# A sliding-window attention branch rewritten with transposed probabilities, 64-row score tiles, list scheduling and early weights on the SyncE queue

## The chip, the cores and the metric

One core of a Trainium2 chip. The metric is the device time of one execution in microseconds (us); executions of one kernel agree within about 1% here. Engine names: PE is TensorE (PEld the loading of its weights), DVE VectorE, ACT ScalarE, POOL GpSimd, SP SyncE.

## The reference, cut to what matters

Two branches read the same input and are mixed by a gate.

```python
g = sigmoid((x * gate_w).sum(-1, keepdims=True))          # x: 1 x 2048 x 640
a = A_ref(x, wqkv, wo)      # 32 heads of 20, each query sees itself and 255 keys before it
b = B_ref(x, mem0, Wq, Wk, Wv, Wo, seg_len=32)   # 64 segments in sequence, 32 heads of 192, 8 memory rows
return g * a + (1 - g) * b
```

The change touches branch A alone, and how branch B's weights get into the chip while A runs.

## The kernel before

It has four stages: branch A over 16 query blocks of 128 rows; projections of the tails for branch B; the recurrence of branch B; the mix. Branch A walks the heads in a fixed order. Scores stand with queries on the partitions, so the probabilities must be transposed on PE and evacuated before they meet V:

```python
def st_scores(h):
    for ci, c in enumerate(kbs):                       # up to 3 key blocks
        nc.tensor.matmul(sp[...], lhsT=qm[r][:, g, :], rhs=kring[c][:, g, :], start=True, stop=not need_mask)
        if need_mask:                                  # 2 of the 3
            nc.tensor.matmul(sp[...], lhsT=ident[:], rhs=(m_last if c == qb else m_first)[:], start=False, stop=True)
    nc.vector.tensor_reduce(out=nmx[:], in_=sp[:, 0:nk * P], axis=AX.X, op=ALU.max, negate=True)
    nc.scalar.activation(out=ex[:, 0:nk * P], in_=sp[:, 0:nk * P], func=ACT.Exp, bias=nmx[:], scale=1.0)

def st_transpose(h):                                   # two heads at a time
    nc.tensor.transpose(pt_ps[:, a, ci, :], ex[:, ci * P:(ci + 1) * P], ident[:])
    ...                                                # copied out by ACT or DVE in turn
# ... values, output projection ...
early, late, last = weights.resident[:34], weights.resident[34:-3], weights.resident[-3:]
units = [lambda u=u: weights.load_resident(pre, u, nc.gpsimd) for u in early]
units += [lambda u=u: weights.pack(u, nc.gpsimd) for u in streamed]
```

`qm` are copies of Q in which all but one of four heads are zero. A "unit" loads one 384 KB weight tile of branch B, or packs one from DRAM to DRAM for later streaming; those of Wo are packed by four DMAs of 80 KB.

## Time and profile before

| stage | from, us | to, us | what limits it |
|---|---|---|---|
| branch A | 0 | 526 | order of coupled engines, PE most loaded |
| tail projections | 526 | 706 | PE, with one long store |
| recurrence | 706 | 2541 | PE and streamed weights |
| mix | 2541 | 2571 | small |

The median was 2569.75 us of 3 runs. The stage bounds are starts of the first instruction of a stage in the trace. The lines that carry the reading are in the prediction below.

### The profile page before, as it was taken

The page shows a single profiled execution, that of the slowest core. Times are in us where ns is not written, and L with a number is a line of the kernel's source. Part 1 is how long each engine was busy: PE and PEld are TensorE (multiplying, and loading weights), DVE is VectorE, ACT ScalarE, POOL GpSimd, SP SyncE. Part 2 cuts the span into 40 slices and gives each one's busy share as a digit, 9 for nine tenths or more (in the row PEclk, how much of TensorE's full clock was granted, in tenths as well). Part 3 has the DMA queues.
Part 4 walks back from the last instruction along what each step waited for, and adds up shares of the span by engine and source line. Part 5 has one row for each costly group of instructions (what it writes and reads, how often), then busy time and mean ns, then how long its engine had stood idle before and what let it go on. Part 6 is the DMA issues. An engine that isn't in the chain of part 4 may idle for free.

```text
span 2571.1 us, 114087 instructions
## 1 busy us (share of the span) xinstructions
PE 2226.3 (87%) x49877; PEld 1645.7 (64%) x49893; DVE 1198.7 (47%) x3578; ACT 1124.3 (44%) x2433; POOL 702.2 (27%) x1973
## 2 busy tenths in 40 slices
PE   7889888889889888888888888888888888889885
PEld 5777777679456665666656666656666566566663
DVE  5777777623234443444444344434443344344434
ACT  4777777622234333433333343333333343333333
POOL 7622222040122222222222222222222222222220
PEclk9999999899999999999999999999999999999996
DMA  6600000075578888888888888888888888888887
GB/s 210 202 17 18 17 17 15 9 252 148 144 242 277 265 263 263 276 266 278 269 259 269 271 275 266 264 256 270 265 266 270 255 268 273 268 266 270 268 258 228
DMA packets 293747, 561.63 MB, mean 218 GB/s; under 512 B 104568, under 2 KB 114048, under 8 KB 293248
## 3 DMA queue, kind: packets, MB, share of 16 engines
q1 hardware_dynamic: 266032, 495.28, 60.5%
q0 software_dynamic: 24256, 55.62, 7.3%
q8 instruction: 391, 6.41, 1.0%
q10 hardware_dynamic: 2960, 3.44, 0.4%
q14 instruction: 108, 0.88, 0.1%
HBM read 524.83 MB, written 36.51 MB: 218 GB/s over the span
## 4 chain that ended last, share of the span: by engine, by line
PE 53%; DMA 33%; ACT 9%; DVE 2%; issue 2%; SPq 0%; ACTq 0%; POOL 0%; DVEq 0%
DMA t_w<-w_packed 30%; PE ps_o L771 8%; PE ps_k L601 7%; PE ps_q L601 7%; PE ps_v L601 6%; ACT a_ex L195 4%; PE t_psum L440 4%; ACT a_pt L208 3%; PE qk_ps L124 3%; PE ps_pv L747 3%; PE tr_k L616 2%; PE t_psv L457 2%; PE S_ps L673 1%; PE pt_ps L205 1%; PE s_ps L187 1%
## 5 line engine op out<-in xcount | busy, mean ns | idle before, releaser
L601 PEld LDWEIGHTS <-t_hT 128*32 128x32 bf16 x15360 | 381.5, 98 | 292.3 <-issue 70.3
L771 PE MATMUL ps_o<-t_OT,t_w 128*128 128x40 bf16 x7040 | 290.5, 180 | 116.0 <-DMA t_w<-w_packed 108.7
L771 PE MATMUL ps_o<-t_OT,w_o 128*128 128x40 bf16 x8320 | 320.8, 180 | 48.0 <-ACT t_OT L752 45.2
L771 PEld LDWEIGHTS <-t_w 128*128 128x128 bf16 x7040 | 226.3, 96 | 136.9 <-DMA t_w<-w_packed 133.5
L771 PEld LDWEIGHTS <-w_o 128*128 128x128 bf16 x8320 | 267.0, 96 | 58.0 <-issue 48.4
L195 ACT ACTIVATE a_ex<-s_ps,a_nmx 128x384 bf16<-128x384 f32 (+2 forms) x512 | 252.8, 576 | 64.4 <-DVE a_nmx L193 64.2
L648 POOL COPY t_K<-t_xqk 128x64 bf16<-128x64 bf16 x256 | 60.9, 238 | 779.6 <-PE S_ps L673 779.6
L193 DVE TENSOR_REDUCE a_nmx<-s_ps 128x1 f32<-128x384 f32 (+2 forms) x512 | 247.0, 523 | 34.7 <-PE s_ps L190 25.4
L601 PE MATMUL ps_v<-w_v,t_hT 128*32 128x384 bf16 x4864 | 254.6, 337 | 0.1
L752 ACT CAST t_OT<-ps_pv 128x480 bf16<-128x480 f32 x256 | 143.2, 559 | 251.6 <-PE ps_pv L747 247.9
L601 PE MATMUL ps_q<-w_q,t_hT 128*32 128x384 bf16 x4096 | 223.0, 340 | 18.7 <-DVE t_hT L782 18.4
L639 DVE COPY t_K<-tr_k 128x256 bf16<-128x256 bf16 x256 | 74.6, 291 | 344.7 <-PE tr_k L616 344.4
L601 PE MATMUL ps_k<-w_k,t_hT 128*32 128x384 bf16 x4096 | 221.8, 339 | 0.0
L606 ACT CAST t_tok<-ps_k 128x384 bf16<-128x384 f32 x256 | 122.7, 479 | 206.3 <-PE ps_k L601 206.3
L625 ACT COPY b_QT<-tr_q 128x384 bf16<-128x384 bf16 x256 | 123.3, 482 | 180.1 <-PE tr_q L616 180.1
L730 DVE TENSOR_TENSOR t_PTx<-PT_ps,mk_x 128x320 bf16<-128x320 f32 x256 | 125.9, 492 | 153.2 <-PE PT_ps L723 153.1
L606 ACT CAST t_tok<-ps_q 128x384 bf16<-128x384 f32 x256 | 122.6, 479 | 145.8 <-PE ps_q L601 145.8
L683 DVE TENSOR_REDUCE sm_mx<-S_ps 128x4 f32<-128x160 f32 x256 | 82.2, 321 | 209.6 <-PE S_ps L673 209.0
L187 PE MATMUL s_ps<-KT_blk,QTm 128*128 128x128 bf16 x1440 | 172.0, 224 | 5.8 <-ACT a_ex L195 5.4
L606 ACT CAST t_vtok<-ps_v 128x384 bf16<-128x384 f32 x256 | 122.7, 479 | 103.7 <-PE ps_v L601 103.7
L561 POOL DMA_DIRECT2D t_xqk<-xbqk x256 | 137.4, 537 | 84.0 <-POOL b_QT L629 39.1
L205 PE MATMUL pt_ps<-a_ident,a_ex 128*128 128x128 bf16 x1440 | 146.4, 221 | 8.3 <-ACT a_ex L195 1.0
(138 smaller groups left out, 4469.2 us busy)
## 6 DMA issues: line engine op xcount, KB each, us to landing
t_w<-w_packed SPq DMA_DIRECT2D x704, 320.0 KB, 4.2
t_w<-w_packed SPq DMA_DIRECT2D x576, 384.0 KB, 4.4
xbqk<-t_qk SPq DMA_DIRECT2D x16, 768.0 KB, 4.3
t_xqk<-xbqk POOLq DMA_DIRECT2D x256, 48.0 KB, 3.7
w_v<-in_B_Wv_dram POOLq DMA_DIRECT2D x19, 384.0 KB, 8.2
w_q<-in_B_Wq_dram POOLq DMA_DIRECT2D x16, 384.0 KB, 5.2
w_k<-in_B_Wk_dram POOLq DMA_DIRECT2D x16, 384.0 KB, 6.9
xbv<-t_vt SPq DMA_DIRECT2D x64, 96.0 KB, 1.8
```

The source lines that it names most:

```text
L187: nc.tensor.matmul(sp[:, ci * P:(ci + 1) * P], lhsT=qm[r][:, g, :], rhs=kring[c][:, g, :], start=True, stop=not need_mask)
L193: nc.vector.tensor_reduce(out=nmx[:], in_=sp[:, 0:nk * P], axis=AX.X, op=ALU.max, negate=True)
L195: nc.scalar.activation(out=ex[:, 0:nk * P], in_=sp[:, 0:nk * P], func=ACT.Exp, bias=nmx[:], scale=1.0)
L205: nc.tensor.transpose(pt_ps[:, a, ci, :], ex[:, ci * P:(ci + 1) * P], ident[:])
L440: nc.tensor.matmul(pt[:, bb, :], lhsT=ws[ki][kt][:, c:c + P], rhs=xTb[:, kt, t * P:(t + 1) * P], start=(kt == 0), stop=(kt == KT - 1))
L561: sc.op("DMA", 500, lambda: nc.gpsimd.dma_start(tile_of(qk)[:].rearrange("p i b t -> p (i b t)"), xbqk[s, :, g].rearrange("p i c -> p (i c ...
L601: nc.tensor.matmul(t[32 * j:32 * j + 32, 0:384], lhsT=tile_of(hT)[:, kt, :], rhs=w[:, j * 384:(j + 1) * 384], start=(kt == kts[0]), stop=( ...
L606: sc.op("ACT", act(384), lambda: nc.scalar.copy(tile_of(tok)[:], b["tile"][:, 0:384]), reads=[b], writes=[tok])
L625: nc.scalar.copy(dst, tq["tile"][:].rearrange("p b (j t) -> p b j t", t=SEG))
L730: nc.vector.tensor_tensor(out=tile_of(dst)[:], in0=PT["tile"][:, i, :, :].unsqueeze(2).to_broadcast([P, 2, 4, L]), in1=mk.unsqueeze(1).uns ...
L752: sc.op("ACT", act(480), lambda: nc.scalar.copy(tile_of(OT)[:].rearrange("p b j l -> p (b j l)"), o["tile"][:, 0:480]), reads=[o], writes= ...
L771: nc.tensor.matmul(t[:, dt * L:(dt + 1) * L], lhsT=w[:, r * D + dt * P:r * D + (dt + 1) * P], rhs=OT["tile"][:, b, i, :], start=(g == 0 an ...
```

## The change

Its intent: compute the scores twice. The first pass has queries on the partitions and gives only the maximum of each row; the second has keys on the partitions, so that its exponentials are already the transposed probabilities that the value matmul wants as weights. The maximum is put into Q as two additional rows through an augmentation matmul. Heads lie in pairs within 64 rows, so that a score matmul uses half of PE's rows; each matmul of the first pass is issued next to one of the second, 22 heads behind, in the other half. All of branch A goes through the list scheduler that branch B had: a part of the program that takes the operations with their estimated lengths and, of those that are ready, emits the one of highest rank next.

```diff
-    nc.tensor.matmul(sp[...], lhsT=qm[r][:, g, :], rhs=kring[c][:, g, :], ...)
-    nc.tensor.matmul(sp[...], lhsT=ident[:], rhs=(m_last ...)[:], start=False, stop=True)
-    nc.vector.tensor_reduce(out=nmx[:], in_=sp[...], axis=AX.X, op=ALU.max, negate=True)
-    nc.tensor.transpose(pt_ps[:, a, ci, :], ex[...], ident[:])
+    nc.tensor.matmul(T(out)[:, i * P:(i + 1) * P], lhsT=b if keys_first else a, rhs=a if keys_first else b,
+                     start=True, stop=True, tile_position=(r, 0))          # r = 64 * (h % 4 // 2)
+    nc.vector.tensor_tensor_reduce(out=T(junk)[:, 0:n], in0=T(s)[:, 0:n], in1=mask[...], op0=ALU.add, op1=ALU.max, ...)
+    nc.scalar.activation(out=T(pt)[:, h % 4, 0:n], in_=T(s)[:, 0:n], func=ACT.Exp)
+    nc.gpsimd.affine_select(out=v, in_=v, compare_op=op, fill=0.0, ...)    # the mask, 2 for 4 heads
 ...
+    sc = Sched(..., make, stay=300)
+    LAG1, LAG2, BURST, AUG = 22, 30, 2, 2
 ...
-    early, late, last = weights.resident[:34], weights.resident[34:-3], weights.resident[-3:]
-    units = [lambda u=u: weights.load_resident(pre, u, nc.gpsimd) for u in early]
+    early, late, last = weights.resident[:29], weights.resident[29:-3], weights.resident[-3:]
+    units = [lambda sc, u=u: sc.op("DMA", 500, lambda: weights.load_resident(pre, u, nc.sync)) for u in early]
+    units += [lambda sc, u=u: sc.op("DMA", 500, lambda: weights.pack(u, nc.sync)) for u in streamed]
```

## The prediction

> **What bounds the kernel now.** I first split the span into stages by busy time per stretch; each engine name is followed by its busy microseconds and its instruction count.
>
> ```profile
> 0.00:60.00 60.00, 41.95 (x556) 33.54 (x558) 32.09 (x100) 27.86 (x78) 46.27 (x90) 0.94 0.63 201
> 60.00:100.00 40.00, 35.36 (x556) 28.88 (x554) 30.39 (x72) 30.49 (x64) 23.60 (x48) 0.96 0.80 276
> 100.00:500.00 400.00, 350.82 (x5687) 298.53 (x5698) 295.44 (x650) 293.96 (x562) 97.90 (x211) 0.94 0.09 24
> 526.00:706.00 180.00, 162.31 (x2240) 140.32 (x2239) 50.78 (x81) 43.20 (x80) 39.50 (x89) 0.97 0.65 187
> 706.00:2550.00 1844.00, 1608.40 (x40483) 1124.04 (x40483) 762.90 (x2630) 702.08 (x1607) 494.98 (x1537) 0.97 0.84 265
> ```
>
> The columns are PE, PEld, DVE, ACT, POOL, granted clock, DMA share and GB/s. The sliding branch takes the first 526 us, the projections of the tails the next 180, the memory recurrence 1844, the final mix about 20. The change rewrites only the first stage and its hand-off to the second. The page's chain is dominated by work of the recurrence, so it says nothing about this change; 526 us is all that can shrink.
>
> Inside the first stage I read the groups of instructions, shapes kept apart, between 100 and 500 us (some 12.5 query blocks):
>
> ```profile
> L195 ACT ACTIVATE a_ex<-s_ps,a_nmx 128x384 bf16<-128x384 f32 x391 | 201.3, 596 | 53.7 <-DVE a_nmx L193 53.5
> L193 DVE TENSOR_REDUCE a_nmx<-s_ps 128x1 f32<-128x384 f32 x392 | 199.5, 548 | 29.9 <-PE s_ps L190 21.4 <-remote 5.1 <-issue 0.2
> L187 PE MATMUL s_ps<-KT_blk,QTm 128*128 128x128 bf16 x1176 | 138.0, 225 | 4.2 <-ACT a_ex L195 4.2
> L205 PE MATMUL pt_ps<-a_ident,a_ex 128*128 128x128 bf16 x1169 | 114.0, 221 | 5.9
> L190 PE MATMUL s_ps<-m_first,a_ident 128*128 128x128 bf16 x392 | 88.4, 226 | 0.0
> L190 PE MATMUL s_ps<-m_last,a_ident 128*128 128x128 bf16 x392 | 88.1, 225 | 0.0
> L208 ACT COPY a_pt<-pt_ps 128x768 bf16<-128x768 bf16 x98 | 79.6, 812 | 25.4 <-PE pt_ps L205 25.0
> ```
>
> Per head there are 3 score, 2 mask and 3 transpose matmuls, one maximum, one exponential and half an evacuation of transposes. The durations overlap, so cost is better taken from start-to-start spacing in the trace: 56 ns for a 128-column matmul, 25 ns for the 21-column value matmuls. A block then needs on PE (96 + 64 + 96 + 80 + 10) x 56 = 19.4, values 96 x 25 = 2.4, V and output projections 2.7, together 24.6 us. The chain of waits shows what a block really takes:
>
> ```profile
> 262.94 2.44 PE out_ps L255 x9
> ...
> 278.63 0.81 ACT a_pt L208
> 279.49 0.31 PE o_ps L221 x6
> ...
> 286.44 1.91 ACT a_ex L195 x4
> ...
> 295.50 0.63 PE out_ps L255
> ```
>
> The same output projection returns after 32.6 us, and in between the chain hops PE, ACT, DVE. DVE and ACT are each busy about 74%. So no engine is full: the stage is bound by a fixed order of coupled engines with PE the most loaded (24.6 of 31 to 33 us).
>
> **What the Trainium skill says.** "TensorEngine Tiling (Array Packing)", Key Properties: a change of tiling mode drains TensorE, and tiles run in parallel. The trace agrees: a 128-row transpose followed by a column-tiled matmul starts 149 ns later instead of 56, and column-tiled score matmuls of the recurrence start 3 ns apart. Row tiles, which the change uses, do not occur before; "TensorE: Matmul & The Clock Gate", Measured speedup vs the span model, gives 3.07x for four. "VectorE: DVE Perf Modes", the perf-mode tier table, gives tensor_tensor no speed-up with a PSUM operand; the recurrence's 320-element one is spaced 407 ns, which agrees (333 at one element a cycle plus 74). "DMA: Bandwidth & Descriptors", HWDGE ordering: descriptors of one queue are consumed in ring order on each DMA engine. No row of the kernel before tests this, and my largest correction rests on it.
>
> **The change part by part.** Scores are computed twice, by query for the maximum and by key for the probabilities. This removes mask matmuls, probability transposes, their evacuations and the eight zero-padded Q tiles. The maximum goes back into Q through an augmentation matmul; masking goes into the DVE reduction and into POOL selects.
>
> PE per full block: 96 pairs of 64-row matmuls, the partners in opposite row halves, at 56 + 3 = 59 ns: 5.7; values 2.4; Q and K projections 80 x 56 = 4.5; V and output 2.7; transposes 0.6; augmentation 2 x (216 + 4 x 56) = 0.9; gate 0.1. That is 16.9. The order of instructions of the new kernel has 32 to 48 mode changes in a full block (counted from its PE list); 40 at about 95 ns (149 - 56, rounded up) are 3.8. PE: 20.7 us.
>
> DVE: the maximum is now an operation on two tensors, written as two instructions: 407 + 64/0.96 = 474, plus about 66 for the small second one (the spacing of one-column operations before): 540. Times 32: 17.3. K copies 0.9, normalisation 1.2, the rest 0.8: 20.2 us.
>
> ACT: an exponential without a bias tile is spaced 221 ns at 160 elements in the recurrence, so 221 + 224/1.2 = 408 at 384 (463 to 475 before). Times 32: 13.1. Evacuations of Q, K, V, augmented Q and outputs: 5.1. Together 18.2 us, from about 23.
>
> POOL: 16 selects of 512 elements at about 0.6 us (its 512-element copy took 0.61) plus 2.7: 12.3 us, not critical.
>
> Three engines sit between 18 and 21 us. A list-scheduled order with deeper buffers will not fill one wholly; the recurrence, ordered this way, keeps PE about 87% busy (1608 of 1844). I choose 23.5 us per full block, 88% of the PE sum.
>
> **The opening** matters as much. In the new SyncE order, input blocks 0 and 1 are followed by 29 weight loads of 384 KB, 9 packings of 384 KB and 44 of 80 KB, and only then by input block 2. That is 11.4 + 3.5 + 3.6 = 18.5 MB. The new PE order transposes input block 2 after only some 24 heads of block 0, and PE is in order, so everything stops there. About 3.6 MB of inputs go first, by 12 us (the first 10 us before moved 255 GB/s). Weight loads then at some 320 GB/s (268 at a DMA share of 0.84, scaled to a full share): 36 us; packings between DRAM places at an estimated 250 to 280: 27 us. Input block 2 lands near 75 us, while PE reaches it near 30. In the kernel before these weights went through POOL's queue and the input did not wait behind them.
>
> **Sum of the stage:** 75, plus 20 for the rest of blocks 0 and 1, plus 14 x 23.5 = 329, plus 14 for the drain (exponentials lag the maxima by 22 heads, 9 us, then values and output) = 438 us, against 526: minus 88.
>
> **Hand-off.** Five fewer resident weights are early (29, not 34), so 5 x 384 KB = 2 MB more load after the stage. The chain there shows
>
> ```profile
> 526.09 6.87 PE t_psum L440 x120
> 532.96 0.02 issue
> 532.99 0.59 ACT t_qk L445
> 533.58 0.02 issue
> 533.60 21.03 DMA xbqk<-t_qk
> ```
>
> a small-packet store that takes 21 us while the late weights load, against 4.3 us in the median. At 380 GB/s (the busiest late-load stretch) 2 MB are 5 us more of that crowd; I count 4. The new order of resident weights puts all Q and K but three early, as before, so no other wait appears. The recurrence and the mix keep their instructions.
>
> Total: 2570 - 88 + 4 = 2486 us.
>
> **Rivals.**
> 1. Row halves do not overlap. Then scores cost 192 x 56 = 10.8 instead of 5.7 and PE needs 26 us per block, some 28.5 in practice: plus 14 x 5 = 70, so 2556, within 2%. For it: no row tile in this trace. Against: column tiles overlap here, and partners use different PSUM banks.
> 2. The wait for input block 2 is short or hidden. PE reaches it at 30, so 45 us of wait are at stake; blocks 0 and 1 then run at once and the stage ends near 400: 2448. Against: the SyncE order is explicit.
> 3. The two-instruction maximum is dearer, say 650 ns: DVE becomes the bound at 23.7 and the block 26: plus 35, so 2521.
> 4. The schedule fits so well that PE's 20.7 becomes 21.5: minus 28, so 2458.
> 5. The gain is lost at the hand-off because the late loads crowd more stores: at most one further 21 us store, 2507.
>
> **Range and chances.** Rivals 2 and 4 set the low end, 2445; rival 3 with some of 5 sets the high end, 2535. Faster by over 2% means below 2518, which needs 52 us of the 84 to survive. Rivals 1 and 3 break it: 0.82 faster, 0.16 within 2%, 0.02 slower.
>
> **What would show it.** In the changed kernel: the stage ends near 440 and a full block recurs after 23 to 24 us; PE idles from about 30 to 75 us on the input's DMA; two score matmuls of a pair start a few ns apart; the maximum is spaced about 540 ns on DVE, the exponential about 410 on ACT; the first store of the tail projections still takes about 20 us. The prediction is wrong if pairs are spaced 56 ns each, if DVE is over 95% busy in steady blocks, or if input block 2 lands before 50 or after 100 us.

## The result

The changed kernel took 2500.43 us in the median of 4 runs (2485.29 to 2505.54), the kernel before 2573.47 in the median of 4. The ratio is 0.971, with an interval of 0.966 to 0.976. A ratio here is the mean time of one kernel's fast runs over that of the other's of the same rounds, so not quite the ratio of the medians. In a second set of rounds the unchanged file gave 2495.12 us and 0.969.

Busy time by stretch of the changed kernel (columns as in the prediction):

```profile
0.00:60.00 60.00, 18.08 (x225) 14.26 (x225) 18.45 (x70) 9.08 (x18) 17.78 (x54) 0.79 0.92 334
100.00:400.00 300.00, 286.97 (x5437) 208.90 (x5464) 262.88 (x1020) 249.51 (x577) 168.51 (x367) 0.99 0.09 24
640.00:2460.00 1820.00, 1587.62 (x40135) 1111.12 (x40135) 754.14 (x2599) 694.99 (x1589) 487.36 (x1513) 0.97 0.84 266
```

Branch A ends at 435.8 us instead of 526.1. In its middle PE is now busy 96%, DVE 88% and ACT 83%. The first 60 us are the opposite: PE is busy 18 us of 60, while the DMA engines are full. The recurrence is as it was.

The groups of instructions in the middle, 100 to 400 us, shapes kept apart:

```profile
L356 DVE CUSTOM_DVE_ANT_0 a_junk<-p_s,a_mask 128x384 bf16<-128x384 f32 x431 | 224.5, 553 | 33.9 <-PE p_st L326 26.0 <-PE p_s L326 0.9
L386 ACT ACTIVATE a_pt<-p_st 128x384 bf16<-128x384 f32 x408 | 184.1, 495 | 30.2 <-PE p_st L326 26.7 <-PE p_s L326 0.5
L326 PE MATMUL p_s<-a_k,a_q 64*128 64x128 bf16 x1299 | 130.5, 220 | 0.0
L394 POOL TENSOR_SCALAR_AFFINE_SELECT a_pt<-a_pt 128x512 bf16<-128x512 bf16 x211 | 130.0, 640 | 96.3 <-ACT a_pt L386 95.4
L326 PE MATMUL p_st<-a_qa,a_k 64*128 64x128 bf16 x1276 | 127.1, 218 | 5.8 <-ACT a_pt L386 4.5
L356 DVE DVE_READ_ACCUMULATOR2_ANT a_mx<- 128x1 f32 x431 | 35.4, 82 | 0.0
```

What idles DVE and ACT most is now PE's scores (26.0 of 33.9 and 26.7 of 30.2 us); before, ACT waited for DVE and DVE for PE's scores. The maximum is indeed two instructions.

The opening on the chain of waits, in order of time (start, length, what):

```profile
36.02 8.23 DMA w_packed<-in_B_Wq_dram
44.26 7.74 DMA w_packed<-in_B_Wv_dram
52.55 0.59 SPq L530
...
75.09 0.59 SPq L530
75.80 2.48 DMA a_xt<-in_A_x_dram
78.32 0.71 PE p_m L247 x5
```

The 0.59 us pieces are SyncE issuing one packing DMA of Wo after the other. Only then does it issue the load of input block 2, which lands in 2.48 us and lets PE go on. PE had come to a stop at about 32 us. The hand-off at the end of the stage:

```profile
435.77 7.51 PE t_psum L576 x120
443.28 0.02 issue
443.30 0.60 ACT t_qk L581
443.89 0.02 issue
443.91 26.66 DMA xbqk<-t_qk
```

The same store as before, now 26.66 us instead of 21.03.

The last stretch of the stage, in which only the drain is left, ran at a low granted clock (the third figure from the end):

```profile
400.00:435.00 35.00, 27.62 (x342) 18.08 (x344) 12.01 (x44) 21.16 (x46) 13.32 (x24) 0.55 0.02 6
```

### The profile page after: what moved, and what is told of

The parts are those of the page before. It is cut to its first block, busy times and chain, and to the rows that moved or that the text cites. A ratio compares the mean times of both kernels' runs of the same rounds, so it can differ in the third digit from the quotient of the medians.

```text
span 2483.5 us, 112898 instructions
## 1 busy us (share of the span) xinstructions
PE 2129.7 (86%) x49059; PEld 1521.8 (61%) x49093; DVE 1133.4 (46%) x3942; ACT 1047.4 (42%) x2385; POOL 745.7 (30%) x2097
## 4 chain that ended last, share of the span: by engine, by line
PE 56%; DMA 36%; ACT 3%; issue 2%; SPq 1%; DVE 1%; POOL 0%; ACTq 0%; DVEq 0%; POOLq 0%
DMA t_w<-w_packed 31%; PE ps_k L737 8%; PE ps_q L737 8%; PE ps_o L907 7%; PE ps_v L737 6%; PE t_psum L576 4%; PE p_s L326 3%; PE p_m L281 3%; PE ps_pv L883 2%; PE tr_k L752 2%; PE p_o L410 2%; PE S_ps L809 1%; PE t_psv L593 1%; PE p_st L326 1%; PE tr_q L752 1%
## 5 line engine op out<-in xcount | busy, mean ns | idle before, releaser
L356 DVE CUSTOM_DVE_ANT_0 a_junk<-p_s,a_mask 128x384 bf16<-128x384 f32 (+2 forms) x512 | 253.5, 528 | 45.0 <-PE p_st L326 32.9
L386 ACT ACTIVATE a_pt<-p_st 128x384 bf16<-128x384 f32 (+2 forms) x512 | 220.4, 474 | 89.9 <-PE p_st L326 81.1
L394 POOL TENSOR_SCALAR_AFFINE_SELECT a_pt<-a_pt 128x512 bf16<-128x512 bf16 x240 | 148.0, 639 | 124.5 <-ACT a_pt L386 123.5
L326 PE MATMUL p_st<-a_qa,a_k 64*128 64x128 bf16 x1440 | 150.7, 224 | 10.6 <-ACT a_pt L386 7.3
```

The source lines that it names most:

```text
L326: nc.tensor.matmul(T(out)[:, i * P:(i + 1) * P], lhsT=b if keys_first else a, rhs=a if keys_first else b, start=True, stop=True, tile_posi ...
L356: sc.op("DVE", 135 + n / 0.96, lambda: nc.vector.tensor_tensor_reduce(out=T(junk)[:, 0:n], in0=T(s)[:, 0:n], in1=mask[:, NKB * P - n:], op ...
L386: sc.op("ACT", act_ns(n), lambda: nc.scalar.activation(out=T(pt)[:, h % 4, 0:n], in_=T(s)[:, 0:n], func=ACT.Exp), reads=[s], writes=[pt])
L394: nc.gpsimd.affine_select(out=v, in_=v, compare_op=op, fill=0.0, base=0, pattern=[[0, 4], [sign, P]], channel_multiplier=-sign)
```

## The experiments

Runs e0_after to e4_early24 (none is called e3) were on one chip and e5_spread7 to e8_poolq on another, each set with the kernel before in its own rounds, so totals across the two sets are compared by their ratios.

A rival of the whole gain is the granted clock, which the views above give as 0.94 in the middle of branch A before and 0.99 after. The clock records of the traces settle it: TensorE was granted half its clock in stretches of 3.4 to 6.8 us, 44 of the 400 us before, and in none between 103 and 396 us after. Where no such stretch fell (102 to 195 us), a block before took 31.1 us, so only some 0.7 us of its mean of 31.8 is clock, against a gain of 9.6.

The theory: the gain is the shorter block, which PE bounds and which rests on row halves running side by side; the opening gives some 46 us away to the order on SyncE; the hand-off gives away 5. Rivals: DVE or ACT bound the block; the opening is not exposed, or it is the choice of queue and not of place; the store's time has nothing to do with late weights. The bounds of stages below are read from the traces, and the block's length is that between the transposes of input blocks 4 and 14, over 10.

**Control, e0_after.** No edit.

> Control: the changed kernel as it is. About 2500 us, ratio to before 0.971. In its profile input block 2 is transposed at about 78 us, the stage ends at about 436 us, a full block recurs every 22.4 us. If its clock is lower than in the first profile, the difference of 15 us between its own runs should lie in the stages with dense matmuls and not in the opening.

Measured: 2495.12 us, ratio 0.969. Input block 2 was transposed at 78.4 us, the stage ended at 435.8, a block took 22.19 us: to 0.1 us what the first profile had. The recurrence took 1838.5 us here and 1831.7 there. The tail projections took 188.4 us and 186.2. So the scatter of one kernel lies behind branch A, mostly in the recurrence, and the bounds within branch A can be compared to a fraction of a us as long as no stretch of half clock falls between them. I had expected the opening to be the same, but had tied the scatter to all dense matmuls; those of branch A had no part in it.

**The order of the early weights, e1_spread.** Each load is ordered behind the operation in front of it in the program. This changes only the emitted order; no wait is added.

```diff
-    units = [lambda sc, u=u: sc.op("DMA", 500, lambda: weights.load_resident(pre, u, nc.sync)) for u in early]
+    units = [lambda sc, u=u: sc.op("DMA", 500, lambda: weights.load_resident(pre, u, nc.sync), after=sc.ops[-1:]) for u in early]
```

and the same for `pack`.

> Only the place of the early weight loads in the SyncE order is changed: each is ordered behind the operation in front of it, so they spread over the stage and input block 2 no longer queues behind 18.5 MB. Theory (the opening wait is exposed time): PE does not stop at input block 2, the stage ends near 390 us, total 44 to 48 us less than the unchanged one, about 2454. Rival (the wait is only where the first blocks' latency shows; without it DMA traffic beside the blocks or POOL's tiles take the time back): less than 20 us gained.

Measured: 2444.26 us, ratio 0.948 (0.943 to 0.953), 51 us less than the control in the same rounds. Input block 2 was transposed at 31.7 us instead of 78.4, and the stage ended at 386.6 instead of 435.8. The first 50 us of it, by stretch:

```profile
0.00:50.00 50.00, 35.37 (x484) 25.89 (x484) 32.74 (x147) 21.45 (x63) 25.50 (x73) 1.00 0.39 125
```

PE is busy 35 of 50 us. A block took 22.19 us as before, with loads beside it. The opening was fully exposed time, and traffic beside the blocks cost them nothing that shows. The rival falls. The program tells why the weights had been bunched: it adds a unit every few heads, but a DMA operation without inputs is ready at time 0 for the scheduler, which then emits all of them at the start.

**Row halves, e2_samerows.**

```diff
-        LAG1, LAG2, BURST, AUG = 22, 30, 2, 2
+        LAG1, LAG2, BURST, AUG = 24, 30, 2, 2
```

> The lag between the two score passes is 24 heads instead of 22, so that both partners of a pair use the same half of the rows and cannot run side by side. Theory (overlap of row halves carries the gain on PE, and PE is the bound of a block): partners start 53 to 56 ns apart instead of 3 to 4, PE's sum per block rises by 96 x 52 ns = 5.0 us, a full block takes 26 to 28 us, total +50 to +75, about 2560, so nearly all of the gain over before is gone. Rival (blocks are bound by DVE and ACT, PE has slack): a block below 24 us, total below +25.

Measured: 2550.66 us, ratio 0.991 (0.985 to 0.996). Partners start 56 ns apart in the median (middle half 55 to 66) instead of 4 (3 to 38). A block took 26.73 us, 4.5 more; the stage ended at 494.8, 59 later, of which under 1 us is the drain of two more heads. The middle of the stage, and the same up to and from the block at which the granted clock falls:

```profile
100.00:400.00 300.00, 297.70 (x4671) 227.13 (x4671) 231.34 (x870) 218.31 (x494) 139.65 (x317) 0.94 0.08 21
126.00:277.00 151.00, 149.79 (x2462) 115.13 (x2459) 120.72 (x453) 114.34 (x256) 74.42 (x168) 1.00 0.08 22
277.00:392.00 115.00, 114.19 (x1652) 86.07 (x1652) 81.11 (x304) 78.09 (x173) 49.97 (x112) 0.85 0.07 19
```

PE is full and DVE's and ACT's shares fall. Not all of the 4.5 us is the lost overlap. At full clock, between input blocks 4 and 10, a block took 25.3 us, 3.1 more than the control's 22.3 there; from block 10 to 14 it took 28.8, with two stretches of half clock, 34 us together, of which the control had none. Whether the fuller PE brings them is not shown: e6_pe_add below kept PE as full (279 of 280 us) at a clock of 1.00. From one pair's start to the next it was 56 ns in the median for the control and 111 to 121 here, so PE has 5 to 6 us more to do for 96 pairs, of which 3.1 us, half to 60%, shows in a block. Without the overlap some 30% of the gain is left (0.9% of the time instead of 3.1%), with these slow stretches in it.

**Five fewer early weights, e4_early24.**

```diff
-    early, late, last = weights.resident[:29], weights.resident[29:-3], weights.resident[-3:]
+    early, late, last = weights.resident[:24], weights.resident[24:-3], weights.resident[-3:]
```

> Five fewer resident weights early (24), so five more load after the stage; doubles the step from 34 to 29. Theory: input block 2 lands about 5 us earlier (2 MB at 400 GB/s) and the stage ends 5 us earlier; the first store of the tail projections takes 5 to 6 us more (26.7 to about 32), as it grew from 21.0 to 26.7 with the first five; total within 3 us of the unchanged one. Rival (the store's time is not set by the late weights): the store stays at 27 and the total falls by 5.

Measured: 2495.87 us, as the control (2495.12). Input block 2 came 5.0 us earlier, at 73.4; the stage ended 3.3 us earlier, at 432.5; the first store took 4.3 us more than the control's 26.86:

```profile
440.35 31.16 DMA xbqk<-t_qk
```

The stage's end gained less than the 5.0 us of the input because two stretches of half clock of 3.4 us each, which the control did not have, lengthened two blocks by 1.2 and 1.1 us. Both halves of the trade are there, and the totals agree. At the start of the tail projections, the store's time follows the number of late weights: 21.0 with 27 loaded just then, 26.7 with 32, 31.2 with 37.

**An even spread, e5_spread7.** In e1_spread the step grows as the list shortens, and the last packings followed the last output store onto the chain. The edit is that of e1_spread and

```diff
-            if n >= HA and units and n % max(1, HA * (NB - 2) // (len(units) + 1)) == 0:
+            if n >= HA and units and n % 7 == 0:
```

> As e1_spread, but one weight unit every 7 heads instead of a step that grows as the list gets short, so that no Wo packings pile up behind the last output store (in e1_spread they sat on the chain from 387 to 409 us, after the stage had ended). Theory: the stage still ends near 387 us, the first store of the tail projections starts about 394 instead of 409, total 5 to 15 us below e1_spread, about 2434. Rival (the late loads crowd the store anyway): the store begins earlier but lasts as much longer, within 4 us of e1_spread.

Measured: 2443.01 us, ratio 0.950 (0.946 to 0.954), the same as e1_spread. The packings are gone from the chain, but

```profile
399.19 25.96 DMA xbqk<-t_qk
```

the store, issued 10 us earlier, lasts 10 us longer than e1_spread's 15.55 us (which began at 408.92), because it meets the late loads: it is through at 425.2 us, and at 424.5 in e1_spread. The stage also ended 4 us later, at 390.5; 2.7 us of that is one block with 6.8 us of half clock. The rival held: the late loads set when the store is through.

**More PE work, e6_pe_add.** The first pair of score matmuls of each head is done twice.

```diff
+                    if i == 0:
+                        for m in mms:
+                            m[0]()
-            pe(max(len(m) for m in mms) * 60, f, "s", ...)
+            pe((1 + max(len(m) for m in mms)) * 60, f, "s", ...)
```

> The changed kernel with one more pair of score matmuls per head (the first is done twice, the result is the same): adds about 56 ns x 32 = 1.8 us to PE per block, and the list order then has some 11 more mode changes per block, about 1.0 us more. Theory (PE is the bound of a full block, 20.3 of 22.2 us): a block grows by 2 to 3 us, to 24.2 to 25.2. Rival (DVE or ACT bound, or latency of the order): below 1 us.

Measured, one look: a block took 23.76 us, 1.57 more; the stage ended at 455.7, 19.9 later. Below the 2 to 3 expected, above the rival's 1. The PE order of this run has 726 mode changes in the stage against 616, 7 more per block and not 11, so some 2.5 us were added on PE (an estimate, 32 x 56 ns and 7 x 95 ns), of which 64% showed.

**More DVE work, e7_dve_add.** After each maximum 8 columns are cleared on DVE.

```diff
+            sc.op("DVE", 70, lambda: nc.vector.memset(T(junk)[:, 0:8], 0.0), writes=[junk], after=sc.ops[-1:])
```

> The changed kernel with one small DVE operation more per head (8 columns written), at an estimated 70 to 80 ns of spacing: about 2.4 us of DVE per block, mode changes as before. Theory (PE is the bound, DVE needs 18.3 of 22.2 us): a block grows by less than 1 us, to at most 23.2. Rival (DVE is the bound): it grows by 2 us or more.

Measured, one look: the clears mostly come two at a time, and two maxima with two of them between start 729 ns apart instead of 483, so up to 123 ns each or 3.9 us per block were added, more than planned; a block took 22.81 us, 0.62 more, and the stage ended at 444.7, 8.9 later. Of the added DVE time 16% showed. Taken with e6_pe_add and e2_samerows, PE comes nearest to bounding the block, but none of these edits shows its full cost, so part of a block is still latency between engines. No run added work to ACT alone; its share in this stays open.

**The queue undone, e8_poolq.** The weights go back to POOL's queue, where the scheduler again puts them all at the start.

```diff
-    ... weights.load_resident(pre, u, nc.sync)) for u in early]
+    ... weights.load_resident(pre, u, nc.gpsimd)) for u in early]
```

and the same for `pack`.

> One part of the change undone: the early weights are issued from POOL's queue as before, at the place where the order puts them (all at the start). Theory: input block 2 no longer waits, but POOL is in order and spends 82 issues of about 0.53 us, 43 us or more, before its first selects, so the wait moves to POOL and the first values: the stage ends between 415 and 436 us, total 0 to 20 us below the unchanged one. Rival (the queue was the only trouble): the stage ends near 390 as in e1_spread.

Measured: 2505.01 us, ratio 0.972 (0.967 to 0.977), like the changed kernel. The stage ended at 441.8, later than I expected (415 to 436) and not earlier, with 2.4 us of it from a stretch of half clock. Two stretches of its opening:

```profile
30.00:40.00 10.00, 0.00 (x0) 0.00 (x0) 0.00 (x0) 0.00 (x0) 5.56 (x11) 0.55 1.02 401
60.00:70.00 10.00, 0.00 (x0) 0.00 (x0) 0.00 (x0) 0.00 (x0) 10.00 (x21) 0.50 0.61 164
```

PE, DVE and ACT stand still just as long; now it is POOL that issues weight DMAs until 74 us instead of doing its own work. My expectation had counted only the issue time of 43 us; in the first half POOL issued only one load every 0.97 us, about the time of 384 KB at the 401 GB/s shown, and one every 0.5 us later, so the transfers held it as well. So the queue is not the matter: the place in the order is.

## Why the prediction was right

Predicted were 2486 us, 2445 to 2535, faster by over 2%; measured were 2500 and 2495 in two sets of rounds. The sum of the stage, 438 us, was met within 3 us (435.8), but partly because terms that were off cancel. Point by point:

1. **The opening: 75 us predicted, 78.3 measured; the mechanism right, its terms not.** The prediction had PE stop near 30 us (32) and the input land near 75. The 29 loads were issued from 7.4 to 36.0 us, 29 us at about 400 GB/s instead of 36 at 320 (they landed from 13.9 to 42.8), and the 9 large packings in 9 us. The 44 packings of Wo then took 30.5 us (45.3 to 75.8), though only 3.6 MB: from 50 to 70 us the DMA share was about 0.5, and SyncE started one every 0.635 us. The step "packings between DRAM places at an estimated 250 to 280: 27 us" failed in kind: 39.8 us in all, and most of it is issue time, not bandwidth; the prediction did not say from what the 250 to 280 were estimated. Also, the passage on ring order, on which the prediction rested this wait, had little part in it, for the input did not stand in a ring behind the 18.5 MB: it was issued last, at 75.80, and landed 2.5 us later. It was the issuing engine's order.
2. **A block: 23.5 us predicted, 22.2 measured.** Two of the three sums were too large. The maximum is spaced 473 to 484 ns and not 540: its second instruction starts with the next maximum, runs beside it and adds nothing. So DVE needs about 32 x 0.48 + 2.9 = 18.3 us. The exponential is spaced 371 to 387 ns and not 408. PE's terms held: two thirds of the pairs start 3 to 4 ns apart, one pair follows another after 56 ns in the median (59 assumed), and most mode changes cost 148 to 152 ns instead of 56, so 92 to 96 as assumed (616 of them in the stage, counted from the PE order). If the predicted sum of 20.7 holds, PE is filled to 93% and not 88%.
3. **The rest of blocks 0 and 1: 20 predicted, 24.3 measured; the drain: 14 predicted.** From the transposes of input blocks 3 and 15, 12 blocks took 265.6 us, 22.13 each. With that, 78.3 + 24.3 + 14 x 22.13 leaves 23.4 us for the drain, 9 more than predicted. The prediction took the drain at full clock; the granted clock was 0.55 from 400 to 435 us, with PE busy 27.6 of the 35. How much of the 9 us that explains, no run separates.
   The errors are +3, +4, -19 and +9 us against the sum.
4. **The hand-off: 4 us predicted.** The store grew by 5.6 us, the stage between branch A's end and the recurrence from 180.3 to 186.2. The prediction's sign that this store would still take about 20 us failed (26.7); e4_early24 shows the cause, the number of late weights.
5. **The total.** Between the two profiles the span fell by 87.6 us, against 84 predicted; between the medians by 73 and 83. The recurrence, whose instructions did not change, took between 1824 and 1847 us in the traces. That scatter is larger than the rest of my error.
6. **Small slips in the working.** The block before sums to 24.5 us and not 24.6; 3.6 MB at the 255 GB/s given take 14 us and not 12 (input block 1 landed at 12.8); and 88% is the share of the 23.5 us that the PE sum fills. None moves the result.

The rivals: 1 was tested by e2_samerows and put at plus 70, it is plus 55, part of it at low clock; it did not happen, because row halves do overlap. 2 was put at 2448 with the wait away; e1_spread took 2444. 3 fell with the 473 to 484 ns. 4 happened to about two thirds (22.2 of 23.5 down to 21.5). 5 hardly happened: the hand-off grew by 5.9 us, of which 4 were predicted.

The best kernels are e1_spread and e5_spread7, at ratios of 0.948 and 0.950: the change with its weights spread out.

## What to carry to other kernels

A list scheduler that takes an operation without inputs as ready from the start emits it first; give background loads a place in the order, or an in-order queue will put them ahead of the load that the next block needs. When several engines are brought within 15% of one another, price the block by the most loaded one and a filling share, and check each spacing afterwards: a right total can hide terms that cancel. Do the matmuls of two half-row passes next to each other in opposite halves; pairing them in the same half cost 3.1 us of a 22 us block here at full clock. Before you compare stages of two runs, look whether the granted clock was the same in both.

## What the Trainium skill lacked or had wrong

- The issue time of a DMA on SyncE, which set most of 30 us of the opening: 0.33 us for a 128-row weight load when SyncE had waited before it and 0.43 when it came right behind another; 0.49 and 0.59 for a copy between DRAM places (0.49 for 128 rows as for 64; one every 0.635 us back to back). It belongs to "DMA: Bandwidth & Descriptors", which has a count of sequencer cycles for "previous generations" in a table on trn3, but no time for Trainium2 and none by kind of copy.
- "VectorE: DVE Perf Modes", Two Vector instructions with no wait between them, says that an operation that also writes its accumulator is two instructions, which the trace confirms. It does not say that the second, 82 ns long, adds nothing to the spacing: 473 to 484 ns at 384 elements, against 474 worked out without it.
